# K and x transposed by DMA, groups of batches on the halves of the rows, and 32x32 products on eight tiles of TensorE in a delta-rule attention with two feed-forward blocks

## The chip, the cores and the metric

One core of a Trainium2 chip (trn2). The metric is the device time of one execution in microseconds, lower is better. Of the kernel before, three runs were timed and one execution was profiled.

## The reference, cut to what matters

```python
# q, k, v: (4, 8, 768, 48) float32, beta: (4, 8, 768)
k_n = k / (norm(k, axis=-1) + 1e-6)
for t in range(768):                      # for each of the 32 heads
    y[t]  = q[t] @ state                  # state: 48 x 48, zero at first
    v_old = k_n[t] @ state
    state = state + beta[t] * outer(k_n[t], v[t] - v_old)
x = y as (4 * 768, 8 * 48) = (3072, 384)
x = leaky_relu(x @ w1_in, 0.01) @ w1_out  # w1_in: 384 x 2048, w1_out: 2048 x 384
h = x @ w2_in
out = (h - tanh(h)) @ w2_out              # (3072, 384)
```

## The kernel before, in words

**Work.** The 768 steps are cut into 12 chunks of 64 steps (`n`), two chunks to a unit (`u`, six of them). In a chunk the 32 heads lie as 16 columns of blocks (`m`) on two halves of the 128 rows. Values are float16 pairs (high and low part, index `c`), so each product is three matmuls (high by high, high by low, low by high): `heads` (line 904) issues them for a list of tiles.

Per chunk, the attention is: `keys` (line 976: normalize K, split it into pairs `KN`), `t_batch` (line 1005: K transposed to `KTp`, by 64 matmuls against an identity, `ident2`, and four evacuations of 512 columns from PSUM by ScalarE or VectorE), `g_batch` (line 1016: products K K^T), then per unit `inverses` (line 1051: 30 steps of a triangular solve on VectorE) and `merges` (line 1084: 384 products of 32x32 that join two 32-blocks to a 64-block, on four of the 16 tiles of 32 rows by 32 columns), then per chunk `queries`, `products` (line 1142: K Q^T), `states` (line 1159: the 48x48 states), `outputs` (line 1216: y) and `to_xa` (line 1269: scale y, split it into a pair `w`, and transpose it by 12 matmuls of 128x128 against `ident` and three evacuations to the operand x of the first layer).

In the products with 48 or 64 rows two row halves and two column halves of TensorE work as four tiles (`TILES`); `g` is a group of batches and with it a PSUM bank, `h` the half of the rows, and the product of (`g`, `h`) lands in bank `g`, rows `h ^ g`.

**Feed-forward.** `layer` (line 1398) runs one of the two blocks for one chunk, in eight pieces: `h_part` (line 1312) multiplies by `w_in` into a PSUM bank and applies the activation, `o_part` (line 1340), three pieces behind, multiplies by `w_out`. `layers` (line 31) gives the order: the first blocks of two chunks, then the second blocks of the two chunks before them. This order is the same before and after. All four weights are split into pairs at the start (`weight`, line 831).

**What sets the order.** Nothing runs as written: every step becomes a node of a graph, `schedule` (line 400) plays the nodes through a table of costs with a priority per stage (`BIAS`), and `issue` (line 595) writes out one fixed order for each engine. All matmuls therefore stand on line 599 of the profile and all other instructions on line 602: the groups below go by tile names. Engines and DMA queue work in this order; a step that is late holds all that stands behind it on its engine. All DMAs go through SyncE's queue (SP). Buffers come from rings: `s_r` (tile name `sx`) has 4 buffers of 512 words, `ps_a` 4 PSUM banks for the attention, `ps_h` and `ps_o` two each for the feed-forward.

Of the kernel before, what the change touches and what calls it, by code (L numbers as in the profile page):

```python
# [9 lines left out]
F32 = mybir.dt.float32  # L10
F16 = mybir.dt.float16
# [19 lines left out]
def layers(n):  # L31
# [13 lines left out]
FLIP = range(2,12)  # L45
# [11 lines left out]
    ('dma', 'o_part1', 8): 18.06, ('dma', 'o_part1', 9): 9.55, ('dma', 'products', 1): 36.95,  # L57
    ('dma', 'products', 10): 5.25, ('dma', 'products', 11): 96.31, ('dma', 'products', 2): -155.8,
    ('dma', 'products', 3): 41.69, ('dma', 'products', 4): -3.79, ('dma', 'products', 5): -24.45,
    ('dma', 'products', 6): -45.18, ('dma', 'products', 7): 0.93, ('dma', 'products', 8): 61.71,  # L60
    ('dma', 'products', 9): 0.89, ('dma', 'queries', 0): 44.82, ('dma', 'queries', 1): -122.16,
    ('dma', 'queries', 10): -71.32, ('dma', 'queries', 11): -40.53, ('dma', 'queries', 2): -34.63,
    ('dma', 'queries', 3): -77.29, ('dma', 'queries', 4): -24.44, ('dma', 'queries', 5): 150.11,
    ('dma', 'queries', 6): -71.56, ('dma', 'queries', 7): -10.2, ('dma', 'queries', 8): 144.23,
    ('dma', 'queries', 9): -44.37, ('dma', 'to_xa', 1, 1): 23.55, ('dma', 'to_xa', 3, 1): -44.68,
    ('dma', 'to_xa', 5, 1): 145.3, ('dma', 'to_xa', 7, 1): 80.53, ('dma', 'to_xa', 9, 1): -55.79,
    ('dma', 'v', 0): 113.52, ('dma', 'weight', 0, 0): 97.25, ('dma', 'weight', 0, 1): -35.73,
    ('dma', 'weight', 0, 2): -7.51, ('dma', 'weight', 0, 3): -43.68, ('dma', 'weight', 0, 4): 73.02,
    ('dma', 'weight', 0, 5): -46.78, ('dma', 'weight', 1, 0): 109.1, ('dma', 'weight', 1, 1): -102.85,
    ('dma', 'weight', 1, 2): 133.33, ('dma', 'weight', 1, 3): 94.77, ('dma', 'weight', 1, 4): -97.54,  # L70
    ('dma', 'weight', 1, 5): -230.36, ('dma', 'weight', 2, 0): -69.12, ('dma', 'weight', 2, 1): 4.37,
    ('dma', 'weight', 2, 2): -99.92, ('dma', 'weight', 2, 3): 17.69, ('dma', 'weight', 2, 4): 48.5,
    ('dma', 'weight', 2, 5): 15.25, ('dma', 'weight', 3, 0): 102.88, ('dma', 'weight', 3, 1): 68.29,
    ('dma', 'weight', 3, 2): 31.2, ('dma', 'weight', 3, 3): 33.16, ('dma', 'weight', 3, 4): -26.52,
    ('dma', 'weight', 3, 5): 50.73, ('first_keys', 0): -75.4, ('grams', 0): 39.95, ('grams', 0, 1): 145.57,
    ('grams', 1): -10.62, ('grams', 1, 1): 52.87, ('grams', 10): -20.59, ('grams', 10, 1): 138.09,
    ('grams', 11): 68.81, ('grams', 11, 1): -16.82, ('grams', 2): 24.93, ('grams', 2, 1): 9.26,
    ('grams', 3): 3.37, ('grams', 3, 1): -21.73, ('grams', 4): 154.15, ('grams', 4, 1): 140.02,
    ('grams', 5): -10.12, ('grams', 5, 1): -39.51, ('grams', 6): 118.53, ('grams', 7): -15.64,
    ('grams', 7, 1): 11.46, ('grams', 8): 50.86, ('grams', 8, 1): 8.51, ('grams', 9): -29.95,  # L80
# [6 lines left out]
    ('inverses', 1): 210.44, ('inverses', 1, 1): 27.12, ('inverses', 2): 47.82, ('inverses', 2, 1): 1.25,  # L87
    ('inverses', 3): -122.23, ('inverses', 3, 1): -46.27, ('inverses', 4): 37.9, ('inverses', 4, 1): -78.15,
    ('inverses', 5): 15.64, ('inverses', 5, 1): 88.72, ('keys', 10): -35.12, ('keys', 11): -124.76,
    ('keys', 2): -12.83, ('keys', 3): 22.83, ('keys', 4): -18.31, ('keys', 5): -28.49, ('keys', 6): 31.61,  # L90
    ('keys', 7): -119.04, ('keys', 8): 20.88, ('keys', 9): 63.94, ('merges', 0): 13.71, ('merges', 1): 184.43,
    ('merges', 2): 711.57, ('merges', 3): -7.09, ('merges', 4): 4.94, ('merges', 5): 109.0,
# [6 lines left out]
    ('outputs', 1, 1): 54.8, ('outputs', 10, 1): 43.66, ('outputs', 11, 1): 19.96, ('outputs', 2, 1): 192.47,  # L99
    ('outputs', 3, 1): 7.53, ('outputs', 4, 1): -1.93, ('outputs', 5, 1): 172.92, ('outputs', 6, 1): 14.64,  # L100
    ('outputs', 7, 1): 35.56, ('outputs', 8, 1): 36.4, ('outputs', 9, 1): 55.15, ('products', 0): 16.62,
    ('products', 1): 276.42, ('products', 10): -70.13, ('products', 11): 138.78, ('products', 2): 120.39,
    ('products', 3): 21.99, ('products', 4): -90.65, ('products', 5): 255.79, ('products', 6): 112.74,
    ('products', 7): -14.04, ('products', 8): -7.73, ('products', 9): 178.95, ('queries', 0): -62.0,
    ('queries', 1): -37.25, ('queries', 10): 25.17, ('queries', 11): 32.97, ('queries', 2): 58.55,
    ('queries', 3): -15.55, ('queries', 4): 80.55, ('queries', 5): -159.02, ('queries', 6): -3.3,
    ('queries', 7): 45.58, ('queries', 8): 161.04, ('queries', 9): -100.25, ('states', 0): -87.3,
    ('states', 0, 1): 30.17, ('states', 0, 2): -70.27, ('states', 1): 35.94, ('states', 1, 1): 75.87,
    ('states', 1, 2): -0.95, ('states', 10): 39.35, ('states', 10, 1): 65.74, ('states', 10, 2): 234.36,
    ('states', 11): 60.46, ('states', 11, 1): -140.26, ('states', 2): 41.56, ('states', 2, 1): 7.98,  # L110
# [1397 lines left out]
```

## Time and profile before

| | before |
|---|---|
| three runs | 1012.69, 1011.0, 1012.29 us; median 1012.29 us |
| profiled execution | 1012.05 us, its span 1010.2 us |
| TensorE (PE) matmul busy | 898.1 us, 17452 instructions |
| PE weight loads (PEld) busy | 735.0 us |
| VectorE (DVE) busy | 728.4 us |
| ScalarE (ACT) busy | 618.9 us |
| DMA | 57.63 MB, mean 57 GB/s |

The span runs from the first to the last instruction of the profiled execution; 1.85 us of its own time lie around it. Busy times are averages over stages of different kinds: in the first 126 us the weights are loaded and split and PE has little to do, after that PE is busy nearly all the time. A matmul's record is longer than the distance to the next one, because matmuls are pipelined: what a block of matmuls takes from its neighbours is the distance between the starts of the blocks around it.

### The profile page before, as it was taken

How to read it: one execution, taken by the hardware profiler on the slowest of the kernel's cores; microseconds unless marked ns; L12 is line 12 of the kernel's file. 1: busy time of each engine (PE TensorE's matmuls, PEld its weight loads, DVE VectorE, ACT ScalarE, POOL GpSimd, SP SyncE). 2: the span in 40 equal slices, each digit the busy share in tenths (PEclk: the TensorE clock that was granted, in tenths of full speed). 3: DMA queues.
4: the chain of work that ended last, by engine and by line, in shares of the span. 5: the costliest groups of instructions: out<-in, count | busy, mean ns of one | idle time of the engine just before them, and what ended most of it. 6: DMA issues, size and time to landing. Idle time of an engine off the chain costs nothing.

```text
span 1010.2 us, 38840 instructions
## 1 busy us (share of the span) xinstructions
PE 898.1 (89%) x17452; PEld 735.0 (73%) x17452; DVE 728.4 (72%) x1711; ACT 618.9 (61%) x1374; POOL 4.4 (0%) x21
## 2 busy tenths in 40 slices
PE   2012399899999999999999999999999999999997
PEld 2012388788887778887778887788887778877775
DVE  7999999899999776983889946569744842235432
ACT  6887768888986676572678646547553645243332
POOL 1000000000000000000000000000000000000000
PEclk9999999899999999999999999999999999999999
DMA  9932222442420111000111000101000000000000
GB/s 361 398 107 62 95 58 63 144 125 74 137 70 29 41 44 44 20 16 2 50 50 41 18 2 4 38 18 40 17 4 17 3 18 1 2 2 16 17 12 20
DMA packets 30565, 57.63 MB, mean 57 GB/s; under 512 B 4032, under 2 KB 15296, under 8 KB 30400
## 3 DMA queue, kind: packets, MB, share of 16 engines
q1 hardware_dynamic: 30400, 55.16, 17.0%
q8 instruction: 136, 2.23, 0.9%
q14 instruction: 29, 0.24, 0.1%
HBM read 44.14 MB, written 4.72 MB: 48 GB/s over the span
## 4 chain that ended last, share of the span: by engine, by line
PE 74%; DVE 14%; DMA 5%; ACT 4%; issue 2%; SPq 1%; ACTq 0%
PE ps_o L599 33%; PE ps_h L599 33%; PE ps_a L599 8%; DVE wo L602 2%; ACT sx L602 2%; DMA wo<-in_w_in_dram 2%; DVE gd L602 1%; DVE xi L602 1%; DVE x L602 1%; DVE pq L602 1%; DVE wi L602 1%; DVE g L602 1%; DVE sx L602 1%; DMA qf<-in_q_dram 1%; DMA kf<-in_k_dram 1%
## 5 line engine op out<-in xcount | busy, mean ns | idle before, releaser
L599 PE MATMUL ps_h<-x,wi 128*128 128x256 f16 x3456 | 404.7, 274 | 2.3 <-ACT sx L602 1.2
L599 PEld LDWEIGHTS <-wi 128*128 128x128 f16 x3456 | 334.3, 98 | 49.5 <-issue 3.3
L599 PE MATMUL ps_o<-g,wo 128*128 128x256 f16 x1728 | 205.8, 274 | 0.7 <-DVE g L602 0.5
L599 PE MATMUL ps_o<-wo,g 128*128 128x384 f16 x1152 | 199.7, 326 | 0.5 <-issue 0.4
L602 ACT ACTIVATE g<-sx 128x512 f16<-128x512 f32 x192 | 120.6, 629 | 106.5 <-PE ps_o L599 52.8
L599 PEld LDWEIGHTS <-wo 128*128 128x128 f16 x1728 | 167.0, 98 | 21.6 <-issue 1.0
L599 PEld LDWEIGHTS <-g 128*128 128x128 f16 x1152 | 110.3, 98 | 67.2 <-issue 1.0
L602 DVE SCALAR_TENSOR_TENSOR sx<-sx,kap,ps_h 128x512 f32<-128x512 f32 x96 | 71.2, 745 | 73.7 <-ACT sx L602 73.0
L602 ACT ACTIVATE sx<-ps_h,kap 128x512 f32<-128x512 f32 x96 | 65.0, 680 | 79.6 <-PE ps_h L599 70.1
L602 DVE TENSOR_TENSOR g<-sx,g 128x512 f16<-128x512 f32 x96 | 65.9, 687 | 62.1 <-ACT g L602 61.7
L602 DVE SCALAR_TENSOR_TENSOR g<-sx,g 128x512 f16<-128x512 f32 x96 | 66.0, 689 | 55.4 <-ACT g L602 54.9
L602 ACT ACTIVATE sx<-ps_h 128x512 f32<-128x512 f32 x96 | 56.6, 591 | 50.8 <-PE ps_h L599 34.4
L602 DVE TENSOR_TENSOR gd<-xi 128x30 f32<-128x30 f32 (+9 forms) x180 | 58.8, 327 | 1.8
L602 DVE TENSOR_TENSOR xi<-xi,gd 128x30 f32<-128x30 f32 (+9 forms) x180 | 58.9, 327 | 1.5
L599 PEld LDWEIGHTS <-KTp 48*64 48x64 f16 x3360 | 34.9, 116 | 23.0 <-issue 21.9
L599 PEld LDWEIGHTS <-ones 128*128 128x128 bf16 x124 | 7.7, 100 | 53.9 <-issue 35.9
L602 ACT ACTIVATE jk<-kf 128x48 bf16<-128x48 f32 x160 | 38.4, 240 | 3.5
L599 PEld LDWEIGHTS <-KN 64*64 64x64 f16 x1824 | 20.3, 115 | 23.8 <-ACT KN L602 12.4
L599 PE MATMUL ps_a<-ab,ones 128*128 128x1 bf16 x60 | 8.2, 169 | 30.1 <-DVE n L602 17.1
L602 DVE SCALAR_TENSOR_TENSOR wi<-wo,wi 128x768 int32<-128x768 int32 x32 | 30.2, 953 | 0.1
L602 ACT ACTIVATION_READ_ACCUMULATOR jk<-kf 128x1 f32 x160 | 30.1, 188 | 0.0
L602 ACT ACTIVATE sx<-x,sxs 128x768 f16<-128x768 f32 (+1 forms) x26 | 22.7, 882 | 7.7 <-DVE sxs L602 7.6
(140 smaller groups left out, 1057.4 us busy)
## 6 DMA issues: line engine op xcount, KB each, us to landing
wo<-in_w_in_dram SPq DMA_DIRECT2D x32, 384.0 KB, 7.5
qf<-in_q_dram SPq DMA_DIRECT2D x24, 256.0 KB, 3.3
wi<-in_w_out_dram SPq DMA_DIRECT2D x14, 384.0 KB, 7.2
kf<-in_k_dram SPq DMA_DIRECT2D x12, 384.0 KB, 3.4
vf<-in_v_dram SPq DMA_DIRECT2D x12, 384.0 KB, 3.1
out_dram<-sx SPq DMA_DIRECT2D x48, 96.0 KB, 2.2
x<-in_w_out_dram SPq DMA_DIRECT2D x10, 384.0 KB, 4.7
b<-in_beta_dram SPq DMA_DIRECT2D x6, 512.0 KB, 3.9
```

What stands on the lines that cost most here:

```text
L599: self.eng["pe"].matmul(out=o.real(), lhsT=lhsT.real(), rhs=rhs.real(), start=start, stop=stop)
L602: getattr(self.eng[n.on], op)(**{k: v.real() if isinstance(v, View) else v for k, v in kw.items()})
```

## The change

The change has five parts. For chunks 2 to 11 (`K_DMA`) K is transposed by two DMA transposes from `KN` to `KTp` in place of the matmuls and evacuations of `t_batch`; for chunks 1 to 11 (`X_DMA`) the pair `w` is transposed by two DMA transposes in place of those of `to_xa`. For this the layouts of `KN` and `KTp` change so that a group of batches `g` is a half of the rows of `KTp`, and the products of `g_batch`, `products`, `states` and `outputs` change their tiles with it: row half `g`, column half `h`, bank `g`; the number of products stays. `outputs` is written anew: all Q products, two evacuations of 384 columns, all P products, four additions of 256 or 128 columns, where there were four evacuations of 192 columns and four additions of 64 rows by 192 columns. `merges` of units 2 to 5 (`M8`) spreads its products over eight tiles and two banks. The ring `s_r` has 5 buffers, and every number of `BIAS` is another (left out here, as are the host's layouts of q and out).

```diff
+K_DMA = range(2, 12)
+X_DMA = range(1, 12)
+M8 = range(2, 6)
+SROOMS = 5
+TURNS = 2
...
-    SMALL = ((0.0163, 0.028), (0.0094, 0.0139))
+    SMALL = ((0.0163, 0.028), (0.0094, 0.0139), (0.0065, 0.0139))
...
-    s_r = ring("sx", 4, 512, short=True)
+    s_r = ring("sx", SROOMS, 512, short=True)
...
+    def turn(o, i):
+
+        node = g_.put({"sp": ("dma_start_transpose", dict(out=o, in_=i))}, [o], [i], TURNS * i.ap.free_nbytes() * 128)
+        node.stage = ("dma",) + node.stage
...
-    KN = [fixed(f"KN{i}", [128, NG, 2, GM * D + C - D], F16) for i in range(4)]
-    KTp = [fixed(f"KTp{i}", [128, 2, NM, C], F16) for i in range(3)]
+    KN = [fixed(f"KN{i}", [128, 2, GM, NG, C], F16) for i in range(4)]
+    KTp = [fixed(f"KTp{i}", [128, 2, GM, 2, C], F16) for i in range(3)]
...
     def t_batch(n):
 
-        kn = KN[n % 4]
+        kn, kt = KN[n % 4], KTp[n % 3]
         for c_ in range(2):
+            if n in K_DMA:
+                turn(kt[:, c_].rearrange("p m h i -> p m (h i)"), kn[:, c_].rearrange("p m g d -> p (m g d)"))
+                continue
             ps = banks(C)
             for m in range(GM):
                 for g, h in TILES:
-                    mm(ps[g][HS[h ^ g], m], kn[HS[h], g, c_, m * D:m * D + C], ident2[HS[h]])
-            for g in range(NG):
-                cp(KTp[n % 3][:, c_, g * GM:(g + 1) * GM], ps[g])
+                    mm(ps[h][HS[g], m], kn[HS[h], c_, m, g], ident2[HS[h]])
+            for h in range(2):
+                cp(kt[:, c_, :, h], ps[h])
...
-            k2 = {(g, h): parts(kt, HD[h], g * GM + m) for g, h in TILES}
-            heads([(ps2[g][HS[h ^ g], m], k2[g, h], k2[g, h]) for g, h in TILES])
+            k2 = {(g, h): parts(kt, HD[g], m, h) for g, h in TILES}
+            heads([(ps2[g][HS[h], m], k2[g, h], k2[g, h]) for g, h in TILES])
...
+    def merges8(u, nat, two, tt_, xm):
+
+        HF = [(f, h) for f in range(2) for h in range(2)]
+        g_.quad = 2
+        ps = banks(HB)
+        for m in range(GM):
+            if m == GM // 2:
+                g_.cut()
+            jobs = []
+            for f, h in HF:
+                up, dn, i = HQ[2 * h], HQ[2 * h + 1], m + f * GM
+                jobs += [(ps[f][HQ[2 * (h ^ f) + 1], m], [AT[up, c_, i, 0:HB] for c_ in range(2)], two(nat, up, 2 * i)),
+                         (ps[f][HQ[2 * (h ^ f)], m], [AT[dn, c_, i, HB:] for c_ in range(2)], two(tt_, dn, 2 * i + 1))]
+            heads(jobs)
+        split(PM[:, 0, 0:GM], PM[:, 1, 0:GM], ps[0], 1.0 / KS)
+        for h in range(2):
+            split(PM[HS[h], 0, GM:], PM[HS[h], 1, GM:], ps[1][HS[1 - h]], 1.0 / KS)
...
+        for f in range(2):
+            for a in range(2):
+                for h in range(2):
+                    o = xm[HQ[2 * h], a][:, f * GM:(f + 1) * GM]
+                    split(o[:, :, :, 0], o[:, :, :, 1], ps[f][HQ[2 * (h ^ f) + a]], -1.0 / KS)
...
-            heads([(ps[g][HS[h ^ g], m], parts(kt, HD[h], g * GM + m), parts(Q[:, g], HD[h], m)) for g, h in TILES])
+            heads([(ps[g][HS[h], m], parts(kt, HD[g], m, h), parts(Q[:, h], HD[g], m)) for g, h in TILES])
...
         pt = x.bitcast(F16).rearrange("p (c n) -> p c n", c=2)
-        ps = [g_.tile(ps_a, [128, 512], F32) for _ in range(3)]
...
+        if n in X_DMA:
+            for c in range(2):
+                turn(pt[:, 1 - c].rearrange("p (t n) -> p t n", n=128), w[c])
+        else:
...
```

## Rows read from the trace of the kernel before

**Rows 1.** Windows: length, busy PE, PEld, DVE, ACT, POOL; clock; DMA share, GB/s.

```profile
50.00:126.00 76.00, 20.69 (x1130) 18.27 (x1130) 75.39 (x174) 57.63 (x153) 0.22 (x2) 1.00 0.28 90
126.00:300.00 174.00, 168.40 (x3702) 145.74 (x3702) 167.30 (x393) 144.76 (x378) 0.00 (x0) 0.98 0.32 97
300.00:1004.70 704.70, 700.65 (x12202) 564.11 (x12199) 441.90 (x1017) 377.75 (x715) 0.00 (x0) 1.00 0.08 21
```

**Rows 2.** Instructions on the tile ident after 126 us: count, ns min/median/max, starts.

```profile
L599 PE MATMUL ps_a<-ident,KN x512: 185/193/214, 151.6 to 569.8; 64*64 64x64 f16 x171
L599 PE MATMUL ps_a<-ident,sx x139: 216/219/315, 125.7 to 839.9; 128*128 128x128 f16 x139
```

**Rows 3.** Timeline of PE, 400 to 440 us: start, us, instruction, count.

```profile
415.58 1.15 PE L599 MATMUL ps_o<-g,wo 128*128 128x256 f16 x9
416.66 0.74 PE L599 MATMUL ps_a<-ident,KN 64*64 64x64 f16 x64
417.33 2.14 PE L599 MATMUL ps_h<-x,wi 128*128 128x256 f16 x18
```

**Rows 4.** Timeline of PE, 255 to 300 us.

```profile
256.99 0.39 PE L599 MATMUL ps_a<-ident,sx 128*128 128x128 f16 x4
257.21 1.15 PE L599 MATMUL ps_o<-g,wo 128*128 128x256 f16 x9
258.29 0.44 PE L599 MATMUL ps_a<-ident,KN 64*64 64x64 f16 x32
258.66 2.14 PE L599 MATMUL ps_h<-x,wi 128*128 128x256 f16 x18
...
272.96 1.15 PE L599 MATMUL ps_h<-x,wi 128*128 128x256 f16 x9
273.94 3.11 PE L599 MATMUL ps_o<-g,wo 128*128 128x256 f16 x27
```

**Rows 5.** Timeline of PE, one block of 96 products of merges (unit 5).

```profile
727.43 0.19 PE L599 MATMUL ps_a<-xi,AT 32*32 32x32 f16 x1
...
727.64 0.17 PE L599 MATMUL ps_a<-xi,AT 32*32 32x32 f16 x1
...
728.17 0.18 PE L599 MATMUL ps_a<-XF,AT 32*32 32x32 f16 x1
```

**Rows 6.** Groups by form: shapes, count, busy us, mean ns, idle before.

```profile
L602 ACT ACTIVATE KTp<-ps_a 128x512 f16<-128x512 f32 x37 | 19.9, 596 | 7.4 <-PE ps_a L599 7.2
L602 DVE CAST KTp<-ps_a 128x512 f16<-128x512 f32 x11 | 7.3, 682 | 0.0
L602 ACT ACTIVATE x<-ps_a 128x512 f16<-128x512 f32 x36 | 19.7, 598 | 2.4 <-DVE sx L602 1.5 <-DVE p L602 0.5 <-PE ps_a L599 0.2
L602 DVE SCALAR_TENSOR_TENSOR AT<-ps_a,AT 128x256 f16<-128x256 f32 x24 | 9.7, 415 | 0.3 <-ACT AT L602 0.2
L602 DVE SCALAR_TENSOR_TENSOR XF<-ps_a,XF 32x512 f16<-32x512 f32 x24 | 17.3, 721 | 12.4 <-ACT XF L602 11.8
L602 DVE SCALAR_TENSOR_TENSOR x<-ps_a,qs,x 64x192 f32<-64x192 f32 x44 | 17.0, 422 | 6.8 <-ACT x L602 5.9
```

**Rows 7.** DMA issues: queue, count, KB each, median us to landing.

```profile
qf<-in_q_dram SPq DMA_DIRECT2D x24, 256.0 KB, 3.3
wi<-sx SPq DMA_DIRECT2D x16, 192.0 KB, 2.5
```

**Rows 8.** Chain of waits, 180 to 194 us: start, us, what.

```profile
183.43 2.86 issue
186.92 2.04 PE ps_h L599 x9
188.96 4.60 PE ps_o L599 x27
```

**Rows 9.** Timeline of PE, 362 to 370 us.

```profile
365.14 0.83 PE L599 MATMUL ps_a<-ident,sx 128*128 128x128 f16 x12
...
367.78 2.47 PE L599 MATMUL ps_h<-x,wi 128*128 128x256 f16 x21
```

More of the change, by code (lines that the diff above doesn't have):

```diff
@@ new lines @@
+    ('dma', 'products', 7): 35.6, ('dma', 'products', 8): 93.84, ('dma', 'products', 9): -18.12,
+    ('dma', 'queries', 0): -43.68, ('dma', 'queries', 1): -35.5, ('dma', 'queries', 10): 0.63,
+    ('dma', 'queries', 11): -83.8, ('dma', 'queries', 2): -12.5, ('dma', 'queries', 3): -58.67,
+    ('dma', 'queries', 4): 41.9, ('dma', 'queries', 5): 118.49, ('dma', 'queries', 6): 32.13,
+    ('dma', 'queries', 7): 194.26, ('dma', 'queries', 8): 65.84, ('dma', 'queries', 9): -77.67,
+    ('dma', 'to_xa', 1, 1): 78.4, ('dma', 'to_xa', 10, 1): -0.29, ('dma', 'to_xa', 11, 1): -44.15,
@@ new lines @@
+    ('o_part1', 9): -30.2, ('outputs', 0, 1): 0.44, ('outputs', 1, 1): 110.04, ('outputs', 10, 1): 301.99,
+    ('outputs', 11, 1): 82.13, ('outputs', 2, 1): 209.09, ('outputs', 3, 1): -2.06, ('outputs', 4, 1): 41.51,
+    ('outputs', 5, 1): 70.33, ('outputs', 6, 1): 119.44, ('outputs', 7, 1): 88.94, ('outputs', 8, 1): 19.53,
+    ('outputs', 9, 1): 9.22, ('products', 0): -5.81, ('products', 1): -3.94, ('products', 10): 143.29,
+    ('products', 11): -16.37, ('products', 2): 22.9, ('products', 3): 78.79, ('products', 4): -3.62,
@@ new lines @@
+    ('products', 5): -24.39, ('products', 6): 21.62, ('products', 7): 3.96, ('products', 8): 9.03,
+    ('products', 9): 29.39, ('queries', 0): -92.91, ('queries', 1): -23.52, ('queries', 10): -25.69,
+    ('queries', 11): 63.79, ('queries', 2): -24.25, ('queries', 3): 6.97, ('queries', 4): -11.95,
+    ('queries', 5): 6.05, ('queries', 6): -75.93, ('queries', 7): 48.98, ('queries', 8): 95.74,
+    ('queries', 9): 32.27, ('states', 0): 85.99, ('states', 0, 1): 22.36, ('states', 0, 2): -121.12,
@@ L971, in key_split @@
             tt(kn, kf[:, gs], y[:, gs].unsqueeze(2).to_broadcast([128, GM, D]), ALU.mult)
-            kp = KN[n % 4][:, g, :, 0:GM * D].rearrange("p c (m d) -> p c m d", m=GM)
-            copy(kp[:, 0], kn)
-            tt(kp[:, 1], kn, kp[:, 0], ALU.subtract)
+            kp = [KN[n % 4][:, c_, :, g, 0:D] for c_ in range(2)]
+            copy(kp[0], kn)
+            tt(kp[1], kn, kp[0], ALU.subtract)
     def keys(u):
@@ L1095, in bank2 @@
             return t.rearrange("p (m n) -> p m n", m=NM)
+        xm = tt_.rearrange("p (m a) i c -> p a m i c", a=2)
+        if u in M8:
+            merges8(u, nat, two, tt_, xm)
+            return
         ps = bank2()
@@ L1122, in merges @@
                 split(o[:, :, :, 0], o[:, :, :, 1], ps[HQ[2 * h + a]], -1.0 / KS)
+    def merges8(u, nat, two, tt_, xm):
[14 more added lines that the diff above has]
+            split(PM[HS[h], 0, GM:], PM[HS[h], 1, GM:], ps[1][HS[1 - h]], 1.0 / KS)
+        ps = banks(HB)
+        for m in range(GM):
+            if m == GM // 2:
+                g_.cut()
+            jobs = []
+            for f, h in HF:
+                up, dn, i = HQ[2 * h], HQ[2 * h + 1], m + f * GM
+                jobs += [(ps[f][HQ[2 * (h ^ f)], m], parts(PM, dn, i), two(tt_, dn, 2 * i)),
+                         (ps[f][HQ[2 * (h ^ f) + 1], m], two(nat, up, 2 * i + 1), parts(PM, up, i))]
+            heads(jobs)
+        g_.quad = True
+        for f in range(2):
[3 more added lines that the diff above has]
+                    split(o[:, :, :, 0], o[:, :, :, 1], ps[f][HQ[2 * (h ^ f) + a]], -1.0 / KS)
     q_t, qs_t, p_t = {}, {}, {}
@@ L1174, in states @@
             for m in range(GM):
-                heads([(ps[g][HS[h ^ g], m], parts(kt, HD[h], g * GM + m), parts(SP, HD[h], g * GM + m))
-                       for g, h in TILES])
+                heads([(ps[g][HS[h], m], parts(kt, HD[g], m, h), parts(SP, HD[g], h * GM + m)) for g, h in TILES])
         for g in range(NG):
@@ L1206, in states @@
             for m in range(GM):
-                heads([(ps[g][HS[h ^ g], m], [KN[n % 4][HS[h], g, c_, m * D:m * D + C] for c_ in range(2)], parts(R[:, g], HS[h], m))
-                       for g, h in TILES])
-            for g in range(NG):
-                gs = slice(g * GM, (g + 1) * GM)
+                heads([(ps[h][HS[g], m], parts(KN[n % 4], HS[h], m, g), parts(R[:, g], HS[h], m)) for g, h in TILES])
+            for h in range(2):
+                gs = slice(h * GM, (h + 1) * GM)
                 if zero:
-                    ts(S32[:, gs], ps[g], sc[:, 3:4], None, ALU.mult)
+                    ts(S32[:, gs], ps[h], sc[:, 3:4], None, ALU.mult)
                 else:
-                    stt(S32[:, gs], ps[g], sc[:, 3:4], S32[:, gs], ALU.mult, ALU.add)
+                    stt(S32[:, gs], ps[h], sc[:, 3:4], S32[:, gs], ALU.mult, ALU.add)
     def outputs(n):
@@ L1224, in outputs @@
         ts(sc[:, 4:5], sc[:, 3:4], sv_t[u, s][:, 3:4], KS, ALU.mult, ALU.mult)
-        for k in range(HB2):
-            ps = [g_.tile(ps_a, [128, 512], F32) for h in range(2)]
-            g_.cut()
-            ms = [(t, k * HP + t) for t in range(HP)]
-            jobs = [(t, [(ps[h][HS[g], (t + g * HP) * D:(t + g * HP + 1) * D], parts(Q[:, g], HD[h], m), parts(SP, HD[h], g * GM + m))
-                         for g, h in TILES]) for t, m in ms if n > 0]
-            jobs += [(t, [(ps[h][HS[g], t * D:t * D + D], parts(P[:, g], HS[h], m), parts(R[:, g], HS[h], m))
-                          for g, h in TILES]) for t, m in ms]
-            for j, (t, job) in enumerate(jobs):
-                heads(job, j == 0, j == len(jobs) - 1)
-            for h in range(2):
-                cp(x32[:, k, h], ps[h][:, 0:HP * D], sc[:, 4:5])
-            for h in range(2):
+        xv = x_t[n].rearrange("p (t k f) -> p k t f", t=KT, k=HB2)
@@ new lines, in outputs @@
+        if n > 0:
+            ps = [g_.tile(ps_a, [128, 512], F32) for k in range(HB2)]
+            g_.cut()
+            for h in range(2):
+                for t in range(HP):
+                    i = h * HP + t
+                    heads([(ps[k][HS[w], i * D:i * D + D], parts(Q[:, h], HD[w ^ k], k * HP + t),
+                            parts(SP, HD[w ^ k], h * GM + k * HP + t)) for k, w in TILES])
+            for k in range(HB2):
+                cp(xv[:, k], ps[k][:, 0:DM].rearrange("p (t f) -> p t f", t=KT), sc[:, 4:5])
@@ new lines, in outputs @@
+        ps = [g_.tile(ps_a, [128, 512], F32) for h in range(2)]
+        g_.cut()
+        for k in range(HB2):
+            for t in range(HP):
+                i = k * HP + t
+                heads([(ps[h][HS[w], i * D:i * D + D], parts(P[:, w ^ k], HS[h], i), parts(R[:, w ^ k], HS[h], i))
+                       for h, w in TILES])
+        for h in range(2):
+            src = ps[h][:, 0:DM].rearrange("p (k f) -> p k f", k=HB2)
+            for t in (h, h + 1):
+                f0, f1 = max(128 * t, h * DM // 2), min(128 * t + 128, (h + 1) * DM // 2)
+                o, i = xv[:, :, t, f0 - 128 * t:f1 - 128 * t], src[:, :, f0 - h * DM // 2:f1 - h * DM // 2]
@@ L1238, in outputs @@
                 if n > 0:
[L1239 to L1240 removed]
+                    stt(o, i, sc[:, 4:5], o, ALU.mult, ALU.add)
+                else:
+                    cp(o, i, sc[:, 4:5])
     XT = 2 ** 14
@@ L1274, in to_xa, with turns @@
         pow2_scale(sx[:, 0:1], squares(x), XT)
-        w = [g_.tile(s_r, [128, HB2, DM], F16) for c in range(2)]
-        x3 = x.rearrange("p (k f) -> p k f", k=HB2)
+        w = [g_.tile(s_r, [128, KT * N], F16) for c in range(2)]
         if n in BOTH:
-            copy(w[0], x3, sx[:, 0:1])
-            lo_of(w[1], x3, sx[:, 0:1], w[0])
-        else:
-            for k in range(HB2):
-                copy(w[0][:, k], x3[:, k], sx[:, 0:1])
-                lo_of(w[1][:, k], x3[:, k], sx[:, 0:1], w[0][:, k])
+            copy(w[0], x, sx[:, 0:1])
+            lo_of(w[1], x, sx[:, 0:1], w[0])
+        else:
+            for k in range(2):
+                ks = slice(k * KT * 128, (k + 1) * KT * 128)
+                copy(w[0][:, ks], x[:, ks], sx[:, 0:1])
+                lo_of(w[1][:, ks], x[:, ks], sx[:, 0:1], w[0][:, ks])
         g_.stage = "to_xa", n, 1
         pt = x.bitcast(F16).rearrange("p (c n) -> p c n", c=2)
-        ps = [g_.tile(ps_a, [128, 512], F32) for _ in range(3)]
-        def turn(c, t, o):
-            for k in range(HB2):
-                mm(o[:, k * 128:(k + 1) * 128], w[c][:, k, t * 128:(t + 1) * 128], ident)
-        for c in range(2):
-            g_.cut()
-            for t in range(2):
-                turn(c, t, ps[c][:, t * N:(t + 1) * N])
-            g_.cut()
-            turn(c, 2, ps[2][:, (1 - c) * N:(2 - c) * N])
-            cp(pt[:, 1 - c, 0:2 * N], ps[c])
-        cp(pt[:, :, 2 * N:], ps[2].rearrange("p (c n) -> p c n", c=2))
+        if n in X_DMA:
+            for c in range(2):
+                turn(pt[:, 1 - c].rearrange("p (t n) -> p t n", n=128), w[c])
+        else:
+            ps = [g_.tile(ps_a, [128, 512], F32) for _ in range(3)]
+            def turns(c, t, o):
+                for k in range(HB2):
+                    i = t * HB2 + k
+                    mm(o[:, k * 128:(k + 1) * 128], w[c][:, i * 128:(i + 1) * 128], ident)
+            for c in range(2):
+                g_.cut()
+                for t in range(2):
+                    turns(c, t, ps[c][:, t * N:(t + 1) * N])
+                g_.cut()
+                turns(c, 2, ps[2][:, (1 - c) * N:(2 - c) * N])
+                cp(pt[:, 1 - c, 0:2 * N], ps[c])
+            cp(pt[:, :, 2 * N:], ps[2].rearrange("p (c n) -> p c n", c=2))
         pt = pt.rearrange("p c (t n) -> p c t n", t=KT)
@@ L1470, in lay_out @@
         a.reshape(B, HP, 2, U, 2, C, D).transpose(3, 2, 5, 4, 0, 1, 6)).reshape(U, 128, 2, B * HP, D)
-    qt = q.reshape(B, HP, 2, U, 2, C, D).transpose(3, 4, 2, 6, 0, 1, 5).reshape(U, 2, 2, D, B * HP, C).copy()
-    qt[:, :, :, :, B * HP // 2:] = qt[:, :, ::-1, :, B * HP // 2:].copy()
+    qt = q.reshape(2, B // 2, HP, 2, U, 2, C, D).transpose(4, 5, 0, 7, 3, 1, 2, 6).reshape(U, 2, 2, D, B * HP, C)
     qt = np.pad(qt, ((0, 0),) * 3 + ((0, 64 - D),) + ((0, 0),) * 2)
```

136 lines of the change are left out of this document (58 added, 78 removed), and 29 rows, old and new, of the table BIAS.

## The prediction

> **What bounds the kernel now.** I read the windows of busy time first. Up to 126 us VectorE is the full engine: 75.39 of the last 76 us, while PE works for 20.69 [rows 1]. From 126 to 300 us PE (168.40 of 174) and VectorE (167.30) are both full. From 300 us to the last matmul, at 1004.7, PE is busy for 700.65 of 704.70 us and VectorE for 441.90 [rows 1]. So over 879 us the order gives PE work all the time: idle time of PE is 5.6 + 4.0 us, and what a change takes out of PE's stream between 126 and 1005 us comes off the end, as long as the other engines deliver in time. The chain of waits says the same: it runs through feed-forward matmuls, and its one long gap after 126 us is 2.86 us at 183 us [rows 8]. The price of a block on PE is therefore not its record but what it pushes apart: nine matmuls of the feed-forward start 0.98 us before the next ones (272.96 to 273.94) [rows 4].
>
> **K by DMA.** After 126 us the trace has 512 of the 768 transposing matmuls of K, 64 for a chunk: eight chunks, the last at 569.8 us [rows 2]. The other 256 (chunks 0 to 3) lie in the start, where PE has room; two of these chunks change too, and I cost that at nothing on PE. One chunk in one block: the feed-forward before it starts at 415.58 and hands over 0.98 us later, at 416.56; the next starts at 417.33, so the block takes 0.77 us [rows 3]. Cut in two, it takes 0.47 twice (257.21 + 0.98 = 258.19 to 258.66) [rows 4]; three of the eight were cut. 5 x 0.77 + 3 x 0.94 = **6.7 us** off PE.
>
> **x by DMA.** 139 matmuls against the identity start after 125.7 us [rows 2]; 7 of them are left of chunk 0, which keeps them. The other 132 belong to 11 chunks. Four take 256.99 to 257.21, 55 ns each [rows 4]; they are as wide as the feed-forward's, so no change of tiles is paid. 132 x 0.056 = **7.4 us** off PE.
>
> **Eight tiles in merges.** 384 products a unit, four units, in blocks of 96: 16 blocks. Their number stays, so only their pace counts. In the block shown the 1st starts at 727.43, the 33rd at 727.64, the 96th at 728.17: 6.5 ns each at first, then 530 / 63 = 8.4 ns [rows 5]. The same tiles with the same bank ran faster at first, so the later pace is not what four tiles can do but what PE is fed with; more tiles can help only the first 32. If these go twice as fast, a block gains 0.1 us: 16 x 0.1 = **1.6 us**, which I take. Bounds: nothing, if they don't run side by side, and 96 x 16 x 4.2 ns = 6.4 us, if the whole pace halves.
>
> **Row halves.** The other products keep their number, shapes and two by two tiles; I cost the new tiles at nothing, with one rival below.
>
> **VectorE and ScalarE.** Of the evacuations of K, 37 are on ScalarE (596 ns) and 11 on VectorE (682 ns) [rows 6]; ten of twelve chunks lose theirs, 40 of 48, and eleven chunks lose three evacuations of x on ScalarE (598 ns). So VectorE loses at most all 11, 7.5 us, and ScalarE then 29 x 0.596 + 33 x 0.598 = 37 us. The eight tiles give some back: per unit eight splits of 32 x 256 for four of 32 x 512 (8 x 0.415 - 4 x 0.721 = 0.4 us on VectorE, the price of 256 columns taken from the row on AT), and three smaller splits of PM for one (3 x 0.415 - 0.72 = 0.5), 4 x 0.9 = 3.6 us in all. In `outputs` four additions at 0.422 become two at 0.415 and two of half that width: level. The new evacuations write in strides, which no row here prices; their counts hardly change. After 300 us both engines have room (VectorE is 63% busy) and all this is hidden by PE. Before 300 us VectorE is a bound itself, and its gain is small: three of the 11 casts lie there, 3 x 0.682 = 2 us. I count 0, with 2 as the end.
>
> **The DMA transposes themselves.** 20 of 256 KB and 22 of 192 KB, all on SP's queue, where before none stood; q, v, K and beta loads and the stores of the output queue behind them, and each waits until its pair is split. PE has no part in them. The trace shows no transpose. The nearest rows are a copy of 192 KB within the core's memory, 2.5 us to landing, and a load of 256 KB, 3.3 us [rows 7]; I take these. The path they replace took 417.33 - 416.56 plus two evacuations on each of two engines (2 x 0.6), some 2 us. So K and x come about 1 to 2 us later than before, and the order, planned anew, has to cover that with feed-forward work, of which PE always has some: after 300 us PE idles for 4 us in 705. From below the price is nothing; from above it is the first rival.
>
> **Ring and priorities.** A fifth buffer of `s_r` costs nothing and covers the two that a DMA now holds. The new `BIAS` moves everything; no row prices that. The gap at 183 us and the slow matmuls behind it (36 in 6.64 us, where four times 0.98 is 3.92) cost 2.86 + 2.7 = 5.6 us [rows 4, 8]; the granted clock of the window averages 0.98 [rows 1], so part of it ran at 1.2 GHz, after a gap. This may go, or come elsewhere. In the sum it stays.
>
> **Sum.** 6.7 + 7.4 + 1.6 = 15.7 us. From the profiled execution's 1012.05 us that is **996.4 us**; the median of the runs, 1012.29, lies 0.24 above it, which is inside what a run differs.
>
> **Rivals.**
>
> *Turned data comes late (slower).* PE's order is fixed: where the feed-forward stands behind a product whose K or x has not landed, the whole stream waits. x of one chunk is turned at 365.14 and used at 367.78 [rows 9], so the distance can be short. There are 21 pairs of transposes (10 of K, 11 of x); the gain is gone when each makes PE wait 15.7 / 21 = 0.75 us. At 1.5 us each the time is 1012.05 - 15.7 + 31.5 = 1028 us. For it: a transpose may land much later than a copy, and SP is one queue. Against it: PE idles little now although x comes just ahead of its use, and DMA share after 300 us is 0.08 [rows 1]. Chance 0.13.
> The Trainium skill's Advanced Engine Details and Errata (section "DGE: Hardware vs Software") calls transposes through hardware-made descriptors, as SP's queue makes them, the less efficient way; no run here shows one. By that rule this rival is what comes out.
>
> *VectorE holds the stretch up to 300 us.* There both engines are full, and PE's gain may only turn into waits. Then the gains before 300 us fall away, three chunks of K (two of them cut: 2.7) and three of x (2.0), and only VectorE's own 2 us count: 15.7 - 4.7 + 2.0 = 13.0, so 999 us. Against it: VectorE also works ahead there on chunks that are used later. Chance 0.19.
>
> *More goes.* Without the gap and the slow stretch at 183 us, 15.7 + 5.6: 990.8 us; with an earlier start some 989. For it: there is less small work to bunch up on PE, and ScalarE is 37 us lighter. Against it: the matmuls that bunch up there, merges of unit 1, are not changed. Chance 0.15.
>
> *Banks were the limit.* With a bank for each row half, the other products could pick up speed, at most from 8.4 to 6.5 ns, the two paces of rows 5: six blocks of 96 for each of ten chunks, 5760 x 1.9 ns = 10.9 us more, 985.5 us. Against it: in merges four row groups write one bank at 6.5 ns [rows 5]. Chance 0.03.
> The Trainium skill's TensorEngine Tiling (Array Packing), "Gotcha 1: PSUM Pressure", says that different row tiles cannot use one PSUM bank at the same time. By it the products of K would gain here and the eight tiles, four row groups to a bank, would not. The trace speaks against it.
>
> *It does not do what it says.* If PE's gain comes back as waits elsewhere in the new order, the time stays within 0.2%. Chance 0.05.
>
> **How the numbers follow.** The forecast has 0.45. A change of 0.2%, 2 us, is about what a measurement of this kernel can tell from none. Faster is the forecast with the second, third and fourth rival: 0.45 + 0.19 + 0.15 + 0.03 = 0.82; same 0.05; slower 0.13. The range takes in the cases of gain with their bounds: down to 984 (15.7, 5.6 for the slow stretch, 4.8 more if the eight tiles halve the whole pace, 2 on VectorE, 28.1 in all), up to 1006 (999 and a wait of 0.33 us at each of 21 pairs). Left out are the late turns, the unchanged case and little else.
>
> **What would show it.** K and x: no matmul against the identity after chunk 1's K and chunk 0's x, and 42 transposes in the DMA issues, landing within 4 us; a wait of PE that ends on such a DMA, more than 15 us in sum, makes the forecast wrong. Eight tiles: the block of 96 in merges at 0.65 us from first to last start and not 0.74. VectorE: PE's idle time in the stretch up to 300 us stays near 6 us; if it grows to 10, the second rival is right. Start: PE fills up at about 126 us; if that moves by more than 3 us, the new order and not the five parts made the difference.

## The result, and the profile after

The changed kernel takes 996.43 us (median of 4 runs, 995.13 to 997.34); the kernel before, run beside it, 1012.02 (4 runs, 1011.0 to 1012.69). The ratio is 0.9846, with an interval of 0.9829 to 0.9863: **faster by 15.6 us**, where the prediction had 996.4 us and 15.7. The profiled execution took 995.13 us with a span of 993.4, 16.8 less than that of before.

The page of the changed kernel: span, busy times, DMA packets, the queue that loads instructions, and the DMA transposes with their median time to landing.

```profile
span 993.4 us, 37327 instructions
...
PE 878.6 (88%) x16680; PEld 719.8 (72%) x16680; DVE 717.4 (72%) x1716; ACT 589.3 (59%) x1322; POOL 6.4 (1%) x21
...
DMA packets 69280, 67.11 MB, mean 68 GB/s; under 512 B 42752, under 2 KB 54016, under 8 KB 69120
...
q8 instruction: 130, 2.13, 0.9%
...
x<-sx SPq DMA_TRANSPOSE x22, 2.8
KTp<-KN SPq DMA_TRANSPOSE x20, 3.6
```

772 matmuls are gone from PE (17452 to 16680): 640 of K and 132 of x. The tile `ident` is read for the last time at 128.0 us:

```profile
L603 PE MATMUL ps_a<-ident,KN x128: 209/238/260, 13.4 to 18.8; 64*64 64x64 f16 x128
L603 PE MATMUL ps_a<-ident,sx x12: 265/311/314, 126.3 to 128.0; 128*128 128x128 f16 x12
```

The windows of the changed kernel, in the columns of [rows 1]:

```profile
50.00:126.00 76.00, 16.06 (x991) 14.78 (x990) 74.25 (x173) 50.95 (x142) 0.72 (x2) 1.00 0.36 107
126.00:300.00 174.00, 167.89 (x3508) 144.84 (x3509) 166.95 (x397) 130.11 (x296) 0.00 (x0) 1.00 0.43 111
300.00:988.00 688.00, 685.79 (x11757) 553.12 (x11754) 432.35 (x1021) 367.88 (x752) 0.00 (x0) 1.00 0.13 30
```

The first stage is about as long as before, and VectorE fills it as before. Behind 126 us the end moves by 16.7 us (1004.7 to 988.0): 15.4 are busy time of PE (869.05 in [rows 1], 853.68 here), 1.3 its idle time (9.6 us, now 6.1 + 2.2 = 8.3). Up to 300 us PE idles for 6.1 us, where it was 5.6. The first feed-forward matmuls, before and after:

```profile
128.62 4.16 PE L599 MATMUL ps_h<-x,wi 128*128 128x256 f16 x27
...
129.93 5.48 PE L603 MATMUL ps_h<-x,wi 128*128 128x256 f16 x27
```

They start 1.3 us later than before, and these 27, which take 3.11 us elsewhere, take 1.3 us more than before.

What PE waits for behind 126 us in the changed kernel (total, times, longest), and the one long piece of its chain of waits:

```profile
PE ps_a L603 <- ACT sx L606: 3.5, 2, 3.2
PE ps_a L603 <- issue: 3.1, 2, 3.0
...
PE ps_o L603 <- issue: 0.4, 1, 0.4
...
215.05 2.97 issue
218.02 0.66 PE ps_a L603 x60
218.68 4.04 PE ps_h L603 x36
```

No wait ends on a transpose. The longest, 3.2 us on `sx`, ends at 126.3 us, ahead of the first feed-forward matmul. The waits put down to issue are 3.5 us in sum, before they were 3.7. The gap of [rows 8] has not gone, it stands at 215 us; but the 36 matmuls behind it take 4.04 us, the normal pace, where 36 took 6.64 before. The granted clock of the kernel before was 0.50 there (the level of 1.2 GHz):

```profile
185.40:192.20 6.80, 5.91 (x56) 4.30 (x56) 5.90 (x14) 5.45 (x14) 0.00 (x0) 0.50 0.65 215
```

In the changed kernel it is 1.00 behind the gap. Both gaps are about 2.9 us long and follow small products, so why the clock fell in the one alone no run shows.

### The profile page after: what moved, and what is told of

The parts are those of the page before. It is cut to its first block, busy times and chain, and to the rows that moved or that the text cites. A ratio compares the mean times of both kernels' runs of the same rounds, so it can differ in the third digit from the quotient of the medians.

```text
span 993.4 us, 37327 instructions
## 1 busy us (share of the span) xinstructions
PE 878.6 (88%) x16680; PEld 719.8 (72%) x16680; DVE 717.4 (72%) x1716; ACT 589.3 (59%) x1322; POOL 6.4 (1%) x21
## 4 chain that ended last, share of the span: by engine, by line
PE 70%; DVE 15%; ACT 7%; DMA 4%; issue 3%; SPq 0%; ACTq 0%; DVEq 0%
PE ps_h L603 32%; PE ps_o L603 31%; PE ps_a L603 7%; DVE xi L606 2%; ACT jk L606 2%; DVE wi L606 2%; DVE gd L606 2%; DVE wo L606 2%; ACT sx L606 1%; DVE pq L606 1%; DVE R L606 1%; DVE g L606 1%; DMA wi<-in_w_out_dram 1%; ACT XF L606 1%; DVE XF L606 1%
## 5 line engine op out<-in xcount | busy, mean ns | idle before, releaser
L603 PE MATMUL ps_h<-x,wi 128*128 128x256 f16 x3456 | 409.7, 274 | 1.2 <-ACT sx L606 1.2
L603 PE MATMUL ps_a<-wacc,ones 128*128 128x1 bf16 x64 | 2.7, 165 | 45.8 <-ACT wo L606 42.3
L606 ACT ACTIVATE sx<-x 128x768 bf16<-128x768 f32 x24 | 20.2, 842 | 20.9 <-DVE x L606 20.1
L606 ACT ACTIVATE XF<-ps_a 32x256 f16<-32x256 f32 (+1 forms) x40 | 20.2, 506 | 19.0 <-PE ps_a L603 13.4
```

The lines of the kernel that those rows point to most:

```text
L603: self.eng["pe"].matmul(out=o.real(), lhsT=lhsT.real(), rhs=rhs.real(), start=start, stop=stop)
L606: getattr(self.eng[n.on], op)(**{k: v.real() if isinstance(v, View) else v for k, v in kw.items()})
```

## The experiments

Two questions were open: what each part was worth, and whether the late turn (the rival on the slower side) is far off. The expectations were written before the runs. Times are medians; kernels of one group ran on one chip beside the kernel before, which took 1010.84 us in the group of `m4_same_order`, `fill_early`, `fill_late` and `turn_twice`, 1011.59 in that of the four undone parts, and 1011.43 in the last (`shift_64`, `shift_128`, `block_early`, `turn_k_twice`). Where the runs of a group are set against the changed kernel, the last one has its own stand-in: `shift_128`, with the same work behind 8 us, at 995.96.

### Eight tiles back to four, in the same order

```diff
-(ps[f][HQ[2 * (h ^ f) + 1], m], [AT[up, c_, i, 0:HB] ...
+(ps[f][HQ[2 * h + 1], m], [AT[up, c_, i, 0:HB] ...
```

and so in the five other places of `merges8`.

> The merges' products of the changed kernel on four tiles as before, with the same order of every engine's work; nothing else is altered. Theory: TensorE takes products of 32x32 one per 8.3 ns once the first 32 of a block are out, whatever the tiles, so the block of 96 stays at 0.945 us and the time at 996.4 us, within 1 us. Rival (the term of the prediction): 16 blocks lose 0.1 us each, +1.6 us, and up to +6.4 us if the whole block had gained.

Measured: 993.02 us (992.13 to 993.94), ratio to before 0.9824 (0.9803 to 0.9845). Four tiles lose nothing. They may even win 2 us (0.9824 x 1012.02 = 994.2 against 996.4), but the two intervals overlap, so that is not settled; 1.0 of the 2.6 us between the two spans (993.4 and 990.8) lies ahead of the first feed-forward matmul. A block of 96 in the changed kernel (the 1st, 32nd, 33rd and 96th product):

```profile
559.55 0.18 PE L603 MATMUL ps_a<-xi,AT 32*32 32x32 f16 x1
...
559.66 0.17 PE L603 MATMUL ps_a<-XF,AT 32*32 32x32 f16 x1
559.76 0.17 PE L603 MATMUL ps_a<-xi,AT 32*32 32x32 f16 x1
...
560.29 0.18 PE L603 MATMUL ps_a<-XF,AT 32*32 32x32 f16 x1
```

and the same four with four tiles:

```profile
557.22 0.18 PE L603 MATMUL ps_a<-xi,AT 32*32 32x32 f16 x1
...
557.42 0.17 PE L603 MATMUL ps_a<-XF,AT 32*32 32x32 f16 x1
557.43 0.17 PE L603 MATMUL ps_a<-xi,AT 32*32 32x32 f16 x1
...
557.96 0.18 PE L603 MATMUL ps_a<-XF,AT 32*32 32x32 f16 x1
```

With eight tiles the 32nd product starts 0.11 us after the first, with four 0.20. So eight tiles do take the first 32 faster, as the term supposed. But the 33rd starts 0.21 us after the first in both, and the rest follows at 8.4 ns. All 96 start within 0.74 us either way.

### More work on PE, before and after 300 us

```diff
+if n.stage[0] == "h_part0" and n.stage[1] in range(0, 4):   # fill_late: range(6, 10)
+    k = seen[n.stage] = seen.get(n.stage, -1) + 1
+    if k in (0, 2, 4, 6):
+        for o, lhsT, rhs, _, _ in (n.calls["pe"] * 2)[:12]:
+            self.eng["pe"].matmul(out=o[:, 0:128].real(), lhsT=lhsT.real(), rhs=rhs[:, 0:128].real(), start=True, stop=True)
```

> 16 times 12 matmuls of 128 columns are put in front of pieces of the first layer for chunks 0 to 3, all before 300 us; they write banks that are written over at once, and nothing else is altered. By the records of matmuls of 256 columns (0.112 us) they cost TensorE 16 x 0.67 = 10.7 us. Theory: TensorE sets the end in the stretch from 126 to 300 us too, so the time rises by 9 to 12 us. Rival (VectorE holds the stretch up to 300 us, where it is at work for 166.95 of 174 us): TensorE's added work disappears in its waits, +0 to +6 us.

> The same 16 times 12 added matmuls in front of pieces of the first layer for chunks 6 to 9, where TensorE is at work for 685.8 of 688 us. Theory and rival both expect the whole 10.7 us here (+10 to +12); it is the measure against which the run with the early ones is read.

Measured: 1031.56 us (1030.78 to 1038.05) with the early ones, +35.1 on the changed kernel, and 1019.62 (1017.87 to 1019.87) with the late ones, +23.2. Both theories miss, and the late run, on which all agreed, shows that such an excess comes also where VectorE has room. The waits of PE behind 126 us in the run with early ones:

```profile
PE ps_a L609 <- issue: 19.9, 12, 2.7
```

and with late ones:

```profile
PE ps_a L609 <- issue: 11.9, 8, 2.4
```

against 3.1 + 0.4 us in the changed kernel. "Issue" is a wait for nothing that the profile shows. A new theory came from the page: 130 transfers of kind instruction for 16680 products, 128 products to a transfer (before: 136 for 17452). If PE's instructions come in such pieces, a piece that is used up faster than the next one arrives leaves PE waiting; and 192 added products move every later end of a piece by 192 - 128 = 64 products.

### Sixty-four products more, or 128

```diff
+for _ in range(64):   # shift_128: range(128)
+    self.eng["pe"].matmul(out=o[0:32, 0:1], lhsT=one[0:32, 0:32], rhs=one[0:32, 0:1], start=True, stop=True)
```

ahead of PE's first product; `one` is the operand of ones of that product.

> 64 small products of ones are added ahead of TensorE's first product, where it idles until 7.69 us; they are written over, and the order of all else is unchanged. Theory (TensorE's instructions come in pieces of 128 products, the page's 130 transfers of kind instruction for 16680 products, and a piece that runs in under some 3.6 us leaves TensorE waiting for the next): the pieces now end inside the blocks of small products, where the tuned order had them end among the layers' matmuls. Waits of TensorE put down to issue after 126 us rise from 3.1 us to 15 to 35 us, and the time by 20 to 40 us. Rival (an added product costs its own time alone): 0 to +1 us, and issue waits stay near 3 us.

> The same with 128 added products, twice as many. Theory (pieces of 128 products): every piece ends where it ended in the changed kernel, so the time is that of the changed kernel, 996.4 us within 2, and issue waits stay near 3 us. Rival (what the added products do at the start, their number, is what costs): twice the loss of the run with 64.

Measured: 1028.18 us (1026.45 to 1032.82) with 64 and 995.96 (994.19 to 996.45) with 128. Sixty-four tiny products, at a time when PE idles, cost 32 us; twice as many cost nothing. That excludes both rivals. It is the place of the work in the stream of instructions that counts, and the numbers of products below give the step, 128. Waits of PE behind 126 us, with 64:

```profile
PE ps_a L609 <- issue: 21.4, 13, 3.2
...
PE ps_h L609 <- issue: 3.4, 2, 2.7
```

with 128:

```profile
PE ps_a L609 <- issue: 4.2, 2, 3.5
```

The timeline of PE with 64 added shows one whole piece, from one wait to the next:

```profile
197.65 0.56 PE L609 MATMUL ps_a<-SP,pq 48*64 48x48 f16 x47
198.78 0.59 PE L609 MATMUL ps_a<-SP,pq 48*64 48x48 f16 x49 [0.57 <-issue]
199.30 1.16 PE L609 MATMUL ps_h<-x,wi 128*128 128x256 f16 x9
200.39 0.75 PE L609 MATMUL ps_a<-R,XF 64*64 64x48 f16 x70
203.06 0.40 PE L609 MATMUL ps_a<-R,XF 64*64 64x48 f16 x26 [1.92 <-issue]
```

49 + 9 + 70 = 128 products between the two waits, both in the middle of a block of 96. The piece is used up in some 2.4 us, and the next product comes 4.28 us after the piece began (198.78 to 203.06). A piece of feed-forward matmuls lasts 128 x 0.109 = 14 us (0.98 us for nine), so the next one is there in time. It is the pieces with few such matmuls that wait. Further on, three windows between long waits of the same kernel hold these numbers of products (length, busy PE, the count in brackets, then clock and DMA):

```profile
392.00:538.20 146.20, 143.82 (x2688) 0.99 0.15 35
538.30:585.80 47.50, 46.25 (x1024) 1.00 0.25 48
709.50:719.80 10.30, 8.76 (x256) 1.00 0.01 3
```

21, 8 and 2 times 128. The waits make up 24.8 - 3.5 = 21.3 of the 32 us. The rest goes with the granted clock behind them, 0.97 in the stretch up to 300 us and 0.99 behind it where the changed kernel has 1.00.

This explains the fills. Of +35.1, 10.7 are their own time, 19.9 - 3.5 = 16.4 waits for instructions, and 8 are left for the clock, which was 0.98 behind 300 us there. It also gives the gap of [rows 8] a cause. At 215 us, 36 products of R,KN, nine feed-forward matmuls and most of a block of 96 stand in front of the wait, the same kind of piece. And these windows, from the start into the gap, count the products that PE had taken (x), in the kernel before and in the changed one:

```profile
0.00:184.50 184.50, 85.96 (x3039) 74.08 (x3040) 175.13 (x426) 140.84 (x394) 4.37 (x21) 1.00 0.47 165
...
0.00:216.50 216.50, 111.22 (x3679) 95.71 (x3679) 204.56 (x495) 162.91 (x463) 6.42 (x21) 1.00 0.56 173
```

3039 is 23 x 128 + 95 and 3679 is 28 x 128 + 95. The wait at 203 us with 64 added comes behind 3167 = 24 x 128 + 95. So both gaps stand where a piece ends, and both kernels pay about the same for it (3.7 and 3.5 us): the gain of the change does not come from there.

### One block that keeps step

```diff
+if seen == 4:   # the fourth piece of h_part0 of chunk 2
+    for o, lhsT, rhs, _, _ in (n.calls["pe"] * 128)[:128]:
+        self.eng["pe"].matmul(out=o[:, 0:128].real(), lhsT=lhsT.real(), rhs=rhs[:, 0:128].real(), start=True, stop=True)
```

> 128 added matmuls of 128 columns in one block, ahead of one piece of the first layer of chunk 2, before 300 us; they are written over. Their number keeps the pieces of 128 products in step for all that follows, which the early fill of 16 times 12 did not. Theory (TensorE sets the end before 300 us too): their own time, 128 x 0.056 to 0.073 = +7.2 to +9.3 us. Rival (VectorE holds the stretch up to 300 us): +0 to +3 us.

Measured: 1000.24 us (999.22 to 1001.63), +4.3 on its stand-in and +3.8 on the changed kernel: between the two. Timeline of PE around the block:

```profile
216.61 0.66 PE L609 MATMUL ps_a<-R,KN 64*64 64x48 f16 x60 [1.37 <-issue]
217.21 3.12 PE L609 MATMUL ps_h<-x,wi 128*128 128x256 f16 x27
220.16 7.31 PE L607 MATMUL ps_h<-x,wi 128*128 128x128 f16 x128
227.31 1.15 PE L609 MATMUL ps_h<-x,wi 128*128 128x256 f16 x9
```

The 128 matmuls take 227.31 - 220.16 = 7.15 us, 0.056 each, which is the price that the prediction used for x. The wait ahead of the block is 1.37 us, in the changed kernel 2.97 and in `shift_128` 3.5 in the same place, so some 2 us of the difference lie ahead of the block and are not its work. Its first feed-forward matmul starts at 129.10 us, that of `shift_128` at 130.23, which is 1.1 us more of the same kind. Behind it the windows up to 300 us show no idle time given back:

```profile
126.00:300.00 174.00, 168.24 (x3597) 147.35 (x3595) 160.67 (x383) 124.61 (x284) 0.00 (x0) 1.00 0.41 108
```

PE is idle for 5.8 us (6.1 before the edit), while 6.3 us of VectorE's work (166.95 to 160.67) left the stretch. If VectorE held this stretch, PE's waits would have swallowed the block. So PE sets the pace here too. Between the two profiled executions the sum closes: the last matmul of `block_early` starts 4.1 us later (993.37 against 989.31), and with the 1.1 and 2.1 us won ahead of the block that is 7.3, where the block itself takes 7.15. The medians show less; that other executions differ in what lies ahead of the block is likely, but not shown.

### Turned data later

```diff
 op, kw = n.calls[n.on]
+if op == "dma_start_transpose":   # turn_k_twice: K's alone
+    getattr(self.eng[n.on], op)(**{k: v.real() if isinstance(v, View) else v for k, v in kw.items()})
```

> Each DMA transpose of K and of x is issued twice in a row, so that each turned tile is complete some 3 to 4 us later and SP's queue holds 42 issues of about 1.25 us more. Theory: no wait of TensorE ends on a transpose and the tiles come well ahead of their use, so the time rises by at most 2 us. Rival (turned data comes late): what is behind a transpose waits for it, 21 pairs of K and x by up to 2.8 + 3.6 us less what slack there is, and waits of TensorE that end on such a DMA appear; +16 us at 0.75 us per pair.

> Only the DMA transposes of K are issued twice in a row, so that K's turned tiles are complete some 4 us later; x's are as in the changed kernel. Theory (x's turn stands right between the copy that makes it and the matmuls that use it, K's is made chunks ahead): +0 to +8 us, against the +70.7 us of both doubled. Rival (every transpose delays what stands behind it on SP's queue alike): K's share by number, 20 of 42, some +34 us.

Measured: 1067.15 us (1065.96 to 1067.58), +70.7, and 1013.62 (1010.94 to 1019.81) with K alone, +17.2 on the changed kernel and +17.7 on the stand-in. The cover that the first theory claimed is not there, and the second run lies between its theory and its rival. SP waits for the first transpose of a tile before it issues the second, so each tile is late by more than a landing. The chain of waits of the run with both doubled, at chunk 1's x:

```profile
157.97 3.94 DMA x<-sx
...
161.92 2.77 DMA x<-sx
```

and the timeline of ScalarE and of PE there:

```profile
164.80 0.60 ACT L608 ACTIVATE sx<-ps_h 128x512 f32<-128x512 f32 x1 [8.85 <-DMA x<-sx]
...
165.44 2.13 PE L603 MATMUL ps_h<-x,wi 128*128 128x256 f16 x18 [3.78 <-ACT sx L608]
```

The transpose reads a buffer of the ring `sx`. While it runs, ScalarE has no room to empty PE's PSUM bank `ps_h`, and PE stops. So a transpose that is late does not only hold the matmuls that read its result; it also holds feed-forward work of another chunk, through the ring. PE's waits in that run come to 57 us behind 126 us; 19.9 of them end on a transpose of x itself, 4.1 on one of K. The granted clock was 0.95 up to 300 us and 0.98 behind it, so part of the 70.7 us is the clock.

In the changed kernel both transposes of that x stand at 152.19 us on SP, and ScalarE empties the bank at 157.91:

```profile
152.19 2.83 SPq L606 DMA_TRANSPOSE x<-sx  x2
...
157.91 0.60 ACT L606 ACTIVATE sx<-ps_h 128x512 f32<-128x512 f32 x1 [3.67 <-PE ps_h L603]
```

The second is issued near 153.8 and lands 2.8 us on, near 156.6; the 18 matmuls that stopped in the longer run start at 159.68, and ScalarE needs 0.6 us before them. That is a reserve of some 2.5 us, an estimate from the median landing. The rival on the slower side did not come true, but it was this close.

### The parts undone, with the order written anew

`K_DMA`, `X_DMA` and `M8` were set to `()`, one at a time and all three.

> K of all chunks is turned by products with ident and copies on ScalarE again, all else as in the changed kernel (x by DMA, eight tiles, halves of the rows; the planner writes the order anew). Theory: the 8 chunks after 126 us pay the prediction's term, +6.7 us, or 5 to 8 with the order written anew. Rival (K's products lay in TensorE's gaps): +0 to +2 us.

> x of all chunks is turned by products with ident again, all else as in the changed kernel, with the order written anew. Theory: 132 products of 0.056 us, +7.4 us, or 6 to 9. Rival (x's products lay in gaps, and what the change won is order): +0 to +2 us.

> The switch of the eight tiles is off, all else as in the changed kernel, with the order written anew. Theory: 0 from the products, and what the order written anew brings, -2 to +2 us. Rival (the term of the prediction): +1.6 us, up to +6.4.

> K and x by products, four tiles; what stays of the change is the order of the groups on the halves of the rows and the second layers one pair late. Theory: 6.7 + 7.4 + 0 = +14.1 us, so about 1010.5 us, and the rest of the change (halves, late layers) is worth 0 to 2 us against the kernel before. Rival (the rest of the change carries the gain): +0 to +8 us only.

Measured: 1018.38 us (K on PE, ratio to before 1.0062), 1047.76 (x on PE, 1.0360), 1007.07 (four tiles, 0.9959) and 1059.3 (all three, 1.0478). These are +22, +51, +11 and +63 us on the changed kernel, far above every expectation; all_off is slower than the kernel before (1011.59) by 48 us although the two do nearly the same work. The late second layers that its expectation names are no part of the change: `layers` is the same in both. Four tiles in the same order lost nothing and in the new order 11 us: these runs measure the order, not the parts. That `BIAS` was written for one graph, and lets work meet in the wrong place with any other, is argued from this. With x on PE, the waits of PE behind 126 us begin so, and the granted clock was 0.94 up to 300 us:

```profile
PE ps_a L603 <- ACT sx L606: 7.8, 6, 3.2
```

So what the halves of the rows and the rest are worth could not be taken out of them, and a version of the old kernel with no more than its K and x changed was not tried.

## Why the prediction was right

**PE sets the end from 126 us on: right.** 15.4 of 16.7 us are busy time that PE no longer has. Where the gain lies can be added up in both traces, as the distance from each product's start to the next (at most its record), from the first feed-forward matmul to the last product: 875.8 us before, 858.1 after. Of these 17.7 us, 13.8 stood at the products against the identity (5.8 at K's, 8.0 at x's), 1.8 at the feed-forward's, 0.2 at the other 8819 products, which are as many as before, and 1.9 in waits. The sign for the start held too: the first feed-forward matmul moved by 1.3 us, less than 3.

**K by DMA, 6.7 us, and x by DMA, 7.4 us: right by the traces, not shown by a run of their own.** The price of a 128-column matmul, 0.056 us, was measured by `block_early`. The 640 and 132 matmuls are gone. The two terms give 14.1 us, near the 13.8 of the traces, where the handover behind a block counts with the feed-forward. The runs that undid the parts did not show them, since the order changed with them.

**Eight tiles, 1.6 us: this term was mis-sized; no gain shows.** The step read rightly that the later pace does not depend on the tiles. It then added a gain of 0.1 us from the first 32 products. The rows show these 32 faster by 0.09 us, but the 33rd does not move, so nothing reaches the end. The expected 0.65 us from first to last start is 0.74 as before.

**The slow stretch, left in the sum: part of it went.** The slow matmuls behind the gap, 2.7 us, are gone (36 in 4.04 us); the gap, 2.86 us, only moved to 215 us. "More goes" had both and was half right. But the 2.7 us may belong to the execution and not to the order: of the kernel before, beside the experiments, executions at a granted clock of 1.000 took 1009.0 to 1010.1 us and those at 0.995 took 1013.4 to 1014.1, and the profiled one of the changed kernel (0.999) is the fastest of its four. Other terms stood in no sum: in the traces 1.9 us fewer waits, against 1.3 us for the later start and 1.3 us for the slower first 27 matmuls. 14.1 + 2.7 + 1.9 - 1.3 - 1.3 is 16.1, where the trace has 16.7 and the medians 15.6. The hit to a tenth of a microsecond is luck; that K and x carry the gain is not.

**VectorE holds the stretch up to 300 us: did not come.** Idle time of PE there is 6.1 us, not 10, and an added block was not swallowed.

**The transposes' own cost: near.** They were taken at 2.5 and 3.3 us and landed after 2.8 and 3.6 in the median, 0.3 us more. Four of K's took 4.4 to 6.0 us, over the 4 us that the prediction gave as a sign, and no wait of PE came of it. Packets under 512 B went from 4032 to 42752. The Trainium skill's Advanced Engine Details and Errata says under "DGE: Hardware vs Software" that hardware-made descriptors transpose less efficiently; no run here has the other way beside it, so that is neither shown nor refuted. The next section of that page, "X-Bar Transpose (TRN2)", says that a transpose is as fast as a plain DMA, and the trace agrees to some 0.4 us (2.8 for 192 KB against 2.4 to 2.5 for a copy in the same kernel).

**Turned data comes late: did not come, but was underrated.** The prediction argued from PE's low idle time that the order has slack. The reserve at one x is some 2.5 us, and a delay of one more transpose costs 17 us for K and 71 for both. The price in the rival (the wait itself, 21 times) lacked the buffers that a transpose holds.

**Banks were the limit: no.** In the products SP,KTp of `states` both row halves wrote each bank before, and now each bank has one. A block of 96 takes 0.90 us before and 0.89 after (timelines of PE, 527.05 to 527.95 and 522.07 to 522.96):

```profile
527.05 0.96 PE L599 MATMUL ps_a<-SP,KTp 48*64 48x48 f16 x96
527.95 1.16 PE L599 MATMUL ps_o<-g,wo 128*128 128x256 f16 x9
...
522.07 0.96 PE L603 MATMUL ps_a<-SP,KTp 48*64 48x48 f16 x96
522.96 1.16 PE L603 MATMUL ps_h<-x,wi 128*128 128x256 f16 x9
```

The rule of the Trainium skill's TensorEngine Tiling (Array Packing), "Gotcha 1: PSUM Pressure", that different row tiles cannot use one bank at the same time, has no price that shows here: in `m4_same_order` products of four row groups that write one bank start 6.5 ns apart, the first 32 of a block.

## What to carry to other kernels

Take a matmul that only turns data off a full TensorE by what it pushes apart in the rows around it, and the saving comes out as computed; but measure how long before its use the turned tile lands and which buffer the transpose holds meanwhile. Before crediting faster tiles, look at when the 33rd product of a block starts: if the later pace is the same with more tiles, as here, only fewer products help. An edit that adds or removes matmuls also shifts where the pieces of 128 products end, so test a change in a tuned order with the order held, and with a second version padded by small products, before its price is believed.

## What was not expected

The waits put down to issue: 64 small products at the start cost 32 us and 128 cost nothing. The waits stand where pieces of 128 products end, in the kernel before as well, and behind a piece used up in 2.4 us the next product came 4.28 us after the piece began. That these pieces are the 130 transfers of kind instruction is argued from the counts (130, 131 and 136 for 16680, 16808 and 17452 products); the profile does not tie a wait to a transfer.

The lowest median measured is that of the changed kernel with four tiles in the same order, 993.02 us; that it beats the changed kernel is not settled.
